# Seven head pairs' outputs turned by transposing DMAs instead of TensorE transposes, and rounding splits dealt to other engines

## The chip, the cores and the metric

One NeuronCore of one Trainium2 chip runs the kernel, with its five engines: TensorE (PE, with its weight loads as PEld), VectorE (DVE), ScalarE (ACT), GpSimd (POOL) and SyncE (SP). SP computes nothing here: it issues all of the kernel's DMAs, one after the other. The metric is the device time of one execution in microseconds. Lower is better.

## The reference

Three stages follow each other: attention whose mask lets a query see only the keys of its own cluster, a token and channel mixer, and a second mixer with cosine and sine. The inputs are in single precision.

```python
mask = q_assign[:, :, :, None] == k_assign[:, :, None, :]     # argmax over 16 centroids per head
scores = np.where(mask, scale * q @ k.T, -1e9)
attn = softmax(scores)                                        # B=2, H=8, S=768, D=64
x = (attn @ v).transpose(0, 2, 1, 3).reshape(B, S, H * D)     # B, 768, 512
# moe
h = np.maximum(x.transpose(0, 2, 1) @ w_tok1, 0.0) @ w_tok2   # 768 -> 256 -> 768, over the tokens
u = x + h.transpose(0, 2, 1)
x = u + np.maximum(u @ w_ch1, 0.0) @ w_ch2                    # 512 -> 1536 -> 512, over the channels
# moe2
theta = x @ w_theta
zr, zi = x * np.cos(theta), x * np.sin(theta)
y = einsum('ts,bsd->btd', w_tok_r, zr) + einsum('ts,bsd->btd', w_tok_i, zi)
u = x + y
out = u + np.maximum(u @ w_ch, 0.0)
```

## The kernel before

Products of single precision are made from three matmuls (`mm3`, L174): each operand is split into a high part, rounded to the format that TensorE multiplies fast, and a low part that holds the rest. The product is high by low, low by high and high by high, summed in PSUM. So every operand that a matmul reads has to be rounded (the "h" tile) and subtracted (the "l" tile) by some engine first. `split_sb` (L129) does this from SBUF: its fourth argument names the engine that rounds ("p" POOL at L132, "v" DVE, "a" ACT at L136) and its fifth the engine that subtracts ("p" POOL, otherwise DVE, at L138). A two-letter word such as "av" or "pp" in the code is such a choice. `load_w` (L152) loads a weight of 512 KB that comes as 64-bit numbers, rebuilds single precision from it on ACT (L161), DVE (L164, L165) and POOL (L168, `k_f<-k_f,k_raw` and the like), and splits it. Without a choice of its own a weight is rounded by POOL and ACT in turn and subtracted by POOL.

**Attention.** The 16 heads are taken in eight pairs. A head has three units of two query tiles of 128 rows, so there are 48 units, and the program's loop (L580) goes over them: the scores of unit n (`scores`, PE L491 and L492, then the maximum on DVE and the exponential on ACT), the transposes of unit n-1 (`turn`, L511) and the products with v of unit n-2 (`values`, L532). The outcome is written transposed, channels by tokens, into a tile `xt` (128 channels of a pair by 768 tokens). `natural` (L545) turns it into tokens by channels: six PE transposes (L555, tile `x`) of `xr`, a copy of `xt`, and six multiplications on DVE (L558) that read PSUM and divide by the softmax sums `ri`. `xr` is a copy made by a DMA (`exact`, L124, at L126), from SBUF to SBUF. `natural` runs three units after a pair's last values.

Meanwhile the operands of the heads ahead are made. For a pair, q and k are loaded (`load_pair`), POOL scales q (L438) and splits both (tag "hl", four buffers, so the next pair's split waits until the DMAs that read the last one are through). For each head SP then copies the parts into the shape that the scores need (`prep`, L465): `qh<-qh` twice, `q<-ql`, `k<-kh` twice, `k<-kl`. The cluster masks come as rows 64 to 79 of the second operands `q2` and `k2` (`place`, L450: `q<-m`, `k<-m`, four of 16 rows). In the trace and the lists below q_0, k_0 are those of even heads, q_1, k_1 of odd ones. `qh` and the masks have their buffers back only when the last scores of the head two before are through, so for an even head SP begins about 13.5 us ahead of the first score that needs all of it.

**Between attention and the mixers.** The token mixer needs `nat(b, s)`, the attention's output by tokens, split (`tok_x`, L184, tiles `xh`, `xl`), and the channel mixer needs it transposed. For this `spread` (L205) separates the 16-bit halves of each number (`halves`, L100, tile `xp`), stores them to DRAM (L116, `xtd<-xp`), and `gather` (L211, L214) reads them back with a transposing DMA (DMA_TRANSPOSE, `xc<-xtd`). `tok_up` (L191) makes g and its parts gh (ACT) and gl (DVE, L200), `tok_down` (L219) makes h and adds it to x. `u_split` (L693) splits the result for the channel mixer. The weights of the second mixer's token matmuls are loaded by `load_tok` (L816), 18 of them, named k; products with them are `y`.

**What sets the order.** The program says which tile is made from which. The order of the instructions on each engine, SP's queue included, comes out of a scheduler that simulates the time of every instruction and is fixed when the kernel is built. On the chip each engine works through its list in that order, and an instruction that has to wait holds back all that stand behind it on that engine.

Of the kernel before, what the change touches and what calls it, by code (L numbers as in the profile page):

```python
# [20 lines left out]
P = 128  # L21
# [14 lines left out]
X_AT = (29, 31, 33, 35, 37, 39)  # L36
# [23 lines left out]
def tile_model(ctx: ExitStack, tc: tile.TileContext, qT, kT, v, cent, w1, w2, wc1, wc2, wth, wri, wch, out):  # L60
# [20 lines left out]
    identr = const.tile([P, P], F32R, name="identr")  # L81
    nc.vector.tensor_copy(out=identr, in_=ident)
# [40 lines left out]

    def exact(t, x):  # L124

        nc.sync.dma_start(out=t.bitcast(F32), in_=x)  # L126
        return t
# [106 lines left out]
    with ExitStack() as actx:  # L234
# [235 lines left out]
        xts, xrs = {}, {}  # L470
# [74 lines left out]
        def natural(b, pr):  # L545

            last = (b, pr) == (B - 1, H // 2 - 1)
            sm, xt = sums[b, pr], (xts if last else xrs)[b, pr]
            ri = small.tile([P, NT, 2], F32, tag="ri", bufs=2, name=f"ri{b}{pr}")
            nc.vector.tensor_scalar(out=ri, in0=sm, scalar1=1e-9, scalar2=None, op0=ALU.add)  # L550
            nc.vector.reciprocal(out=ri, in_=ri)
            for q0, n in ((0, 4), (4, 2)):
                ps = ps_t.tile([P, 4, P], F32 if last else F32R, tag="t", name=f"x{b}{pr}{q0}")
                for i in range(n):
                    nc.tensor.transpose(ps[:, i, :], xt[:, (q0 + i) * P : (q0 + i + 1) * P], ident if last else identr)  # L555
                ps = ps.bitcast(F32)
                for i in range(n):
                    nc.vector.tensor_tensor(  # L558
                        out=nat(b, q0 + i)[:, pr * P : pr * P + P].rearrange("p (h d) -> p h d", h=2),
                        in0=ps[:, i, :].rearrange("p (h d) -> p h d", h=2),  # L560
                        in1=ri[:, q0 + i, :].unsqueeze(2).to_broadcast([P, 2, D]),
                        op=ALU.mult,
                    )
# [16 lines left out]
        for n in range(len(units) + SKEW):  # L580
# [42 lines left out]
            if 0 <= n - SKEW:  # L623
# [6 lines left out]
                if h % 2 == 1 and u == NT // 2 - 1:  # L630
                    late.append((n + 3, b, h // 2))
                    if n - SKEW < len(units) - 1:
                        xrs[b, h // 2] = exact(ap.tile([P, S], F32R, tag="xr", bufs=1, name=f"xr{b}{h}"), xts[b, h // 2])
# [27 lines left out]
        for s in range(NT):  # L661
            tok_x(1, s, part, ("av", "ap")[s % 2])
# [30 lines left out]
    def u_split(ch, c):  # L693

        us[ch, c] = h, l = block(f"uh{ch}{c}"), block(f"ul{ch}{c}")
        l = split_sb(h, l, xc[ch][:, c, :], "a", "v")
# [119 lines left out]
    def load_tok(t):  # L816
        wts[t] = [load_w(wri[t][:, j * 512 : j * 512 + 512], f"k{t}{j}") for j in range(2 * NT // 4)]
# [162 lines left out]
```

## Time and profile before

| what | value |
|---|---|
| median of 3 runs | 643.3 us (642.75 to 644.39) |
| the profiled execution | 642.99 us |
| its span | 641.3 us |
| PE busy | 629.2 us (98%) |
| DVE busy | 411.4 us (64%) |
| ACT busy | 356.1 us (56%) |
| POOL busy | 298.1 us (46%) |
| granted clock of TensorE | 9 tenths or more in all 40 slices of the span |
| chain of work that ended last | PE 85%; POOL 4%; DVE 4%; issue 3% |

The span is the stretch from the first to the last instruction that the profile holds; the execution's own time lies 1.7 us above it. Busy times are sums over the span, so an engine with a low share can still be the one that is late in one place. The chain is followed back from the last instruction through what released each step. In the timelines the number in brackets at the end of a row is the time for which the engine had stood idle before that row, and what ended this.

### The profile page before, as it was taken

What the parts mean: (1) busy time and instruction counts of PE and PEld (TensorE: products, weight loads), DVE (VectorE), ACT (ScalarE), POOL (GpSimd) and SP (SyncE); (2) the same over time, 40 slices, a digit from 0 to 9 for tenths busy, and PEclk for the clock granted to TensorE, in tenths of its full rate; (3) what the DMA queues carried; (4) which work ended last, traced back from release to release, by engine and by line L of the source; (5) the groups of instructions that cost most, each with busy time, mean ns of one, the idle gap of its engine ahead of it and who ended that gap; (6) DMA issues with size and microseconds to landing.
All of it is one profiled execution on the core that took longest, in us unless ns stands there. A gap on an engine that the chain in (4) does not pass through costs nothing.

```text
span 641.3 us, 9886 instructions
## 1 busy us (share of the span) xinstructions
PE 629.2 (98%) x3510; PEld 503.7 (79%) x3510; DVE 411.4 (64%) x653; ACT 356.1 (56%) x670; POOL 298.1 (46%) x261
## 2 busy tenths in 40 slices
PE   8999999999999999899999999999999999999997
PEld 6777787777777767788888888888888877888886
DVE  6877777778787758776565442464668977645222
ACT  6766777677778857456433510455767964422110
POOL 8330312309341115437776521492976998644000
PEclk9999999999999999999999999999999999999999
DMA  8655667454698315724433310636061236652331
GB/s 302 171 147 136 173 139 181 120 145 112 182 226 172 108 34 198 163 67 132 132 131 102 127 36 20 177 99 164 2 164 34 85 109 184 182 147 68 88 105 55
DMA packets 65762, 82.02 MB, mean 128 GB/s; under 512 B 40816, under 2 KB 44080, under 8 KB 65712
## 3 DMA queue, kind: packets, MB, share of 16 engines
q1 hardware_dynamic: 65712, 81.39, 46.6%
q8 instruction: 28, 0.46, 0.3%
q14 instruction: 22, 0.18, 0.1%
HBM read 39.65 MB, written 12.06 MB: 81 GB/s over the span
## 4 chain that ended last, share of the span: by engine, by line
PE 85%; POOL 4%; DVE 4%; issue 3%; ACT 2%; DMA 1%; ACTq 0%; POOLq 0%
PE o L532 10%; PE t L511 10%; PE s L491 5%; PE c L180 5%; PE c L178 5%; PE r L178 5%; PE s L492 5%; PE r L180 5%; PE r L179 5%; PE c L179 5%; PE y L178 4%; PE y L180 4%; PE y L179 4%; PE po L179 2%; PE po L180 2%
## 5 line engine op out<-in xcount | busy, mean ns | idle before, releaser
L494 DVE TENSOR_REDUCE nm<-s 128x1 f32<-128x768 f32 x96 | 90.4, 950 | 16.1 <-PE s L492 15.4
L496 ACT ACTIVATE e<-s,nm 128x768 f32<-128x768 f32 x96 | 86.6, 904 | 24.6 <-DVE nm L494 24.2
L511 PE MATMUL t<-ident,e 128*128 128x128 f32 x576 | 84.1, 276 | 0.7 <-ACT e L496 0.4
L511 PEld LDWEIGHTS t<-ident,e 128*128 128x128 f32 x576 | 66.9, 140 | 17.6 <-ACT e L496 6.1
L491 PE MATMUL s<-k,qh 128*128 128x384 f32 x188 | 71.7, 381 | 0.6 <-ACT e L496 0.5
L532 PE MATMUL o<-p,vs 128*64 128x256 f32 x564 | 71.2, 388 | 0.0
L514 ACT ACTIVATE p<-t 128x512 f32<-128x512 f32 x96 | 52.8, 595 | 27.7 <-PE t L511 27.6
L492 PE MATMUL s<-k,q 128*128 128x384 f32 x192 | 64.5, 338 | 0.2 <-ACT k L355 0.2
L178 PE MATMUL y<-zl,k_h 128*128 128x512 f32 x144 | 56.5, 392 | 1.4 <-POOL k_h L132 1.1
L180 PE MATMUL y<-zh,k_h 128*128 128x512 f32 x144 | 56.0, 389 | 0.0
L179 PE MATMUL y<-zh,k_l 128*128 128x512 f32 x144 | 56.0, 389 | 0.0
L179 PE MATMUL r<-uh,c_l 128*128 128x512 f32 x144 | 56.0, 389 | 0.0
L180 PE MATMUL r<-uh,c_h 128*128 128x512 f32 x144 | 55.9, 389 | 0.0
L178 PE MATMUL r<-ul,c_h 128*128 128x512 f32 x144 | 55.4, 389 | 0.0
L532 PEld LDWEIGHTS o<-p,vs 128*64 128x64 f32 x564 | 36.3, 136 | 22.8 <-issue 7.0
L168 POOL TENSOR_TENSOR c_f<-c_f,c_raw 128x512 uint32<-128x512 uint32 x24 | 32.5, 1354 | 40.8 <-issue 19.7
L179 PE MATMUL c<-rh,c_l 128*128 128x512 f32 x128 | 49.8, 389 | 0.0
L180 PE MATMUL c<-rh,c_h 128*128 128x512 f32 x128 | 49.6, 389 | 0.0
L178 PE MATMUL c<-rl,c_h 128*128 128x512 f32 x128 | 49.5, 389 | 0.0
L779 ACT ACTIVATE rh<-r 128x512 fp32r<-128x512 f32 x36 | 20.5, 592 | 49.1 <-PE r L180 49.0
L780 DVE SCALAR_TENSOR_TENSOR rl<-r,rh 128x512 fp32r<-128x512 f32 x36 | 24.4, 687 | 27.4 <-ACT rh L779 27.2
L132 POOL TENSOR_SCALAR qh<-ql 128x768 fp32r<-128x768 f32 x7 | 5.8, 835 | 74.4 <-DMA qh<-qh 70.9
(223 smaller groups left out, 1468.1 us busy)
## 6 DMA issues: line engine op xcount, KB each, us to landing
c_raw<-wc SPq DMA_DIRECT2D x24, 512.0 KB, 3.4
k_raw<-wri SPq DMA_DIRECT2D x18, 512.0 KB, 3.8
qh<-qh SPq DMA_DIRECT2D x28, 192.0 KB, 3.1
k<-kh SPq DMA_DIRECT2D x28, 192.0 KB, 4.1
ql<-qT SPq DMA_DIRECT2D x8, 384.0 KB, 3.2
kl<-kT SPq DMA_DIRECT2D x8, 384.0 KB, 3.7
vs<-v SPq DMA_DIRECT2D x16, 192.0 KB, 2.4
w_raw<-w SPq DMA_DIRECT2D x6, 512.0 KB, 4.1
```

The lines of the kernel that those rows point to most:

```text
L168: nc.gpsimd.tensor_tensor(out=wu, in0=wu, in1=lo, op=ALU.add)
L178: nc.tensor.matmul(ps, ah, bl, start=first and i == 0, stop=False)
L179: nc.tensor.matmul(ps, al, bh, start=False, stop=False)
L180: nc.tensor.matmul(ps, ah, bh, start=False, stop=last and i == n - 1)
L491: nc.tensor.matmul(ps[:, half, :NH], qh[:, c], k1[:, n], start=True, stop=False)
L492: marks["scores"] = nc.tensor.matmul(ps[:, half, :NH], ql[:, c], kk[:, n], start=False, stop=True)
L494: marks["max"] = nc.vector.tensor_reduce(out=nm, in_=ps[:, :, :NH], axis=AX.XY, op=ALU.max, negate=True)
L496: marks["exp"] = nc.scalar.activation(out=e.rearrange("p (a n) -> p a n", a=2), in_=ps[:, :, :NH], func=AF.Exp, bias=nm, accum_out=sums[b, ...
L511: marks["turn"] = nc.tensor.transpose(ps[:, a, i * P : i * P + P], es[i][:, kt * P : kt * P + P], ident)
L514: marks["pA"] = nc.scalar.activation(out=p, in_=ps, func=AF.Copy)
L532: nc.tensor.matmul(po[r : r + 64, :], vs[:, kt, :], pr[kt // 2][:, kt % 2, :], start=kt < 2, stop=kt >= NT - 2, tile_position=(0, r),)
L780: nc.vector.scalar_tensor_tensor(out=l, in0=ps, scalar=0.0, in1=h.bitcast(F32), op0=ALU.max, op1=ALU.subtract)
```

## The change

1. Seven of the eight pairs (all but the last) no longer use PE for `natural`. POOL separates the 16-bit halves of `xt` (`halves` with "p", tile `xh`, 128 x 1536 elements of 16 bits, after's L109), SP stores them to DRAM (`xd<-xh`, after's L114), and in the next turn of the loop at the earliest a transposing DMA reads them back as `xr`, now tokens by channels (`turned_back`, after's L118). The six multiplications by `ri` read `xr` from SBUF and are done by POOL (after's L553). `natural` runs six units after the pair's last values. `xr` has two buffers instead of one.
2. `tok_x` of batch 0 is called for the units 32, 33, 35, 37, 39, 41 (before: 29, 31, 33, 35, 37, 39).
3. In the second batch's `tok_x` DVE subtracts for all six tiles; before, POOL did it for three of them.
4. `u_split` of the first four column tiles (ch 0) subtracts on POOL instead of DVE.
5. The 18 weights of `load_tok` are rounded on ACT and subtracted on DVE; before, nine were rounded by POOL and nine by ACT, and POOL subtracted all 18.

```diff
--- before.py
+++ after.py
@@ -33,7 +33,7 @@
 RAW = 4
 HL = 4
 
-X_AT = (29, 31, 33, 35, 37, 39)
+X_AT = (32, 33, 35, 37, 39, 41)
 GATHERS = (4, 5, 0, 1, 2, 3)
 SPREAD_AT = (43, 44, 45, 46, 47, 48)
 W1_AT = {41: "pp", 43: "pp", 46: "av"}
@@ -78,8 +78,6 @@
     marks = {}
     ident = const.tile([P, P], F32, name="ident")
     make_identity(nc, ident)
-    identr = const.tile([P, P], F32R, name="identr")
-    nc.vector.tensor_copy(out=identr, in_=ident)
     NCH = B * NT // 4
     xc = [const.tile([P, 4, DM], F32, name=f"xc{i}") for i in range(NCH)]
 
@@ -120,11 +118,6 @@
         nc.sync.dma_start_transpose(
             out=t.bitcast(U16).rearrange("p (c q) -> p c q", c=n), in_=rows.rearrange("p t n -> (p t) n")
         )
-
-    def exact(t, x):
-
-        nc.sync.dma_start(out=t.bitcast(F32), in_=x)
-        return t
 
     def split_sb(h, l, x, rnd, sub):
 
@@ -467,7 +460,7 @@
             return qh, q2[i], k1, k2[i], load_v(b, h)
 
         sums = {}
-        xts, xrs = {}, {}
+        xts, xrs, stored = {}, {}, []
 
         def scores(b, h, u, ops):
 
@@ -550,12 +543,14 @@
             nc.vector.tensor_scalar(out=ri, in0=sm, scalar1=1e-9, scalar2=None, op0=ALU.add)
             nc.vector.reciprocal(out=ri, in_=ri)
             for q0, n in ((0, 4), (4, 2)):
-                ps = ps_t.tile([P, 4, P], F32 if last else F32R, tag="t", name=f"x{b}{pr}{q0}")
+                if last:
+                    ps = ps_t.tile([P, 4, P], F32, tag="t", name=f"x{b}{pr}{q0}")
+                    for i in range(n):
+                        nc.tensor.transpose(ps[:, i, :], xt[:, (q0 + i) * P : (q0 + i + 1) * P], ident)
+                else:
+                    ps = xt.rearrange("p (i n) -> p i n", n=P)[:, q0:, :]
                 for i in range(n):
-                    nc.tensor.transpose(ps[:, i, :], xt[:, (q0 + i) * P : (q0 + i + 1) * P], ident if last else identr)
-                ps = ps.bitcast(F32)
-                for i in range(n):
-                    nc.vector.tensor_tensor(
+                    (nc.vector if last else nc.gpsimd).tensor_tensor(
                         out=nat(b, q0 + i)[:, pr * P : pr * P + P].rearrange("p (h d) -> p h d", h=2),
                         in0=ps[:, i, :].rearrange("p (h d) -> p h d", h=2),
                         in1=ri[:, q0 + i, :].unsqueeze(2).to_broadcast([P, 2, D]),
@@ -628,9 +623,17 @@
                         values(group)
                     group = []
                 if h % 2 == 1 and u == NT // 2 - 1:
-                    late.append((n + 3, b, h // 2))
+                    late.append((n + 6, b, h // 2))
                     if n - SKEW < len(units) - 1:
-                        xrs[b, h // 2] = exact(ap.tile([P, S], F32R, tag="xr", bufs=1, name=f"xr{b}{h}"), xts[b, h // 2])
+                        k = f"{b}{h}"
+                        t = halves(ap.tile([P, S], F32, tag="xr", bufs=2, name=f"xh{k}"), xts[b, h // 2], "p")
+                        rows = dram.tile([P, 2, S], U16, tag="xd", bufs=2, name=f"xd{k}")
+                        store(rows, t, nc.sync)
+                        stored.append((n + 1, (b, h // 2), rows))
+            if stored and n >= stored[0][0]:
+                _, k, rows = stored.pop(0)
+                xrs[k] = ap.tile([P, S], F32, tag="xr", bufs=2, name=f"xr{k[0]}{k[1]}")
+                turned_back(xrs[k], rows, NT)
             while late and (n >= late[0][0] or n == len(units) + SKEW - 1):
                 _, b, pr = late.pop(0)
                 natural(b, pr)
@@ -659,7 +662,7 @@
                 ps = ps_o.tile([P, 512], F32, tag="o", name=f"g0{t}")
             tok_up(0, t, ps, lambda name: ap.tile([P, S], F32R, tag="raw", bufs=RAW, name=name)[:, :512])
         for s in range(NT):
-            tok_x(1, s, part, ("av", "ap")[s % 2])
+            tok_x(1, s, part, "av")
         split = marks["h"], marks["l"]
         for s in GATHERS:
             spread(1, s, ap.tile([P, S], F32, tag="hl", bufs=HL, name=f"xp1{s}")[:, :DM], "a")
@@ -693,7 +696,7 @@
     def u_split(ch, c):
 
         us[ch, c] = h, l = block(f"uh{ch}{c}"), block(f"ul{ch}{c}")
-        l = split_sb(h, l, xc[ch][:, c, :], "a", "v")
+        l = split_sb(h, l, xc[ch][:, c, :], "a", "p" if ch == 0 else "v")
         turned[ch] = marks["h"], l
 
     for c in range(NC):
@@ -814,7 +817,7 @@
     wts = {}
 
     def load_tok(t):
-        wts[t] = [load_w(wri[t][:, j * 512 : j * 512 + 512], f"k{t}{j}") for j in range(2 * NT // 4)]
+        wts[t] = [load_w(wri[t][:, j * 512 : j * 512 + 512], f"k{t}{j}", "av") for j in range(2 * NT // 4)]
 
     plan = []
     for t in range(B * NT):
```

Three places in the order of the instructions. A transposing DMA takes a place in SP's list where a plain copy stood. On SP, around the preparation of head 6, the first of the fourth pair (tiles qh, k: first operands; q_0, k_0: second ones; m: masks), the list before has:

```order
L465 DMA qh_1574<-qh_1348 64x768
L126 DMA xr_1446<-xt_936 128x768
L465 DMA qh_1574<-qh_1348 64x768
L465 DMA q_0_145<-ql_1349 64x768
L465 DMA k_1575<-kh_1353 64x768
L465 DMA k_0_147<-kh_1353 64x768
L465 DMA k_1575<-kl_1354 64x768
L450 DMA q_0_145<-m_1523 16x384 x2
L450 DMA k_0_147<-m_1523 16x384 x2
L450 DMA q_1_146<-m_1523 16x384
```

The same stretch of SP's list after the change:

```order
L458 DMA qh_1568<-qh_1329 64x768 x2
L458 DMA q_0_143<-ql_1330 64x768
L458 DMA k_1569<-kh_1334 64x768
L458 DMA k_0_145<-kh_1334 64x768
L458 DMA k_1569<-kl_1335 64x768
L114 DMA xd_1429<-xh_1427 128x1536
L443 DMA q_0_143<-m_1517 16x384 x2
L118 DMA_TRANSPOSE xr_1493<-xd_1429 128x6x256
L443 DMA k_0_145<-m_1517 16x384 x2
L443 DMA q_1_144<-m_1517 16x384
```

The copy to `xr` is gone from among the `qh`; the store `xd` stands behind `k<-kl`, and the DMA that turns it back stands between the two masks of the even head. It reads what the store wrote. Four even heads have this pattern.

The second place is SP's list for head 14, the first of the last pair. Before:

```order
L465 DMA qh_2723<-qh_2489 64x768
L126 DMA xr_2587<-xt_2065 128x768
L465 DMA qh_2723<-qh_2489 64x768
L465 DMA q_0_145<-ql_2490 64x768
L465 DMA k_2724<-kh_2494 64x768
L465 DMA k_0_147<-kh_2494 64x768
L465 DMA k_2724<-kl_2495 64x768
L450 DMA q_0_145<-m_2668 16x384 x2
L450 DMA k_0_147<-m_2668 16x384 x2
```

After, behind two `qh` and one `q_0<-ql`:

```order
L458 DMA k_2702<-kh_2459 64x768
L458 DMA k_0_145<-kh_2459 64x768
L114 DMA xtd_3114<-xp_3112 128x1024
L207 DMA_TRANSPOSE xc_66<-xtd_2941 128x4x256
L207 DMA_TRANSPOSE xc_66<-xtd_3008 128x4x256
L114 DMA xtd_3179<-xp_3177 128x1024
L443 DMA q_0_143<-m_2646 16x384 x2
L443 DMA k_0_145<-m_2646 16x384 x2
L443 DMA q_1_144<-m_2646 16x384
L114 DMA xtd_3214<-xp_3212 128x1024
L207 DMA_TRANSPOSE xc_66<-xtd_3061 128x4x256
L458 DMA k_2702<-kl_2460 64x768
```

`k<-kl`, the last of the six copies that the head's first score reads, has moved behind three stores, three transposing DMAs and five masks. Before, the gathers stood ahead of the head's copies or behind its masks.

The third place is DVE around the second batch's `gl` (L200). Before:

```order
L164 TENSOR_SCALAR c_0_raw<-c_0_f 128x512
L165 SCALAR_TENSOR_TENSOR c_0_f<-c_0_f,c_0_raw 128x512
L138 TENSOR_TENSOR ul_3499<-xc_68,uh_3498 128x512
L138 TENSOR_TENSOR ul_3503<-xc_68,uh_3502 128x512
L138 TENSOR_TENSOR ul_3507<-xc_68,uh_3506 128x512
L138 TENSOR_TENSOR ul_3511<-xc_68,uh_3510 128x512
L164 TENSOR_SCALAR c_1_raw<-c_1_f 128x512
L165 SCALAR_TENSOR_TENSOR c_1_f<-c_1_f,c_1_raw 128x512
L200 SCALAR_TENSOR_TENSOR gl_3534<-g_3514,gh_3533 128x512
```

After:

```order
L131 TENSOR_TENSOR xl_3357<-rest,xh_3356 128x512
L131 TENSOR_TENSOR xl_3361<-rest,xh_3360 128x512
L157 TENSOR_SCALAR c_0_raw<-c_0_f 128x512
L158 SCALAR_TENSOR_TENSOR c_0_f<-c_0_f,c_0_raw 128x512
L157 TENSOR_SCALAR c_1_raw<-c_1_f 128x512
L158 SCALAR_TENSOR_TENSOR c_1_f<-c_1_f,c_1_raw 128x512
L193 SCALAR_TENSOR_TENSOR gl_3504<-g_3484,gh_3503 128x512
```

The four `ul` have left DVE's list, and `gl` follows the weight's rebuilding at once. On POOL's list they stand around the same weight's addition (L168, after's L161).

## Rows read from the trace of the kernel before

**Rows 1.** The page's busy times: engine, busy us, share of the span, instructions.

```profile
PE 629.2 (98%) x3510; PEld 503.7 (79%) x3510; DVE 411.4 (64%) x653; ACT 356.1 (56%) x670; POOL 298.1 (46%) x261
```

**Rows 2.** Busy times by stretch, one pair of heads: stretch and its length, us (instructions), clock, DMA.

```profile
143.19:170.51 27.32, 27.32 (x209) 21.02 (x208) 21.92 (x38) 20.30 (x43) 18.64 (x18) 1.00 0.55 137
```

**Rows 3.** Waits of PE: us in total, times, longest.

```profile
PE h L179 <- DVE gl L200: 2.1, 1, 2.1
PE h L178 <- DVE w_l L138: 1.5, 2, 0.9
...
PE y L178 <- POOL k_h L132: 1.1, 1, 1.1
...
PE y L178 <- POOL zl L138: 0.3, 1, 0.3
```

**Rows 4.** Groups of instructions by line and form, L555: ns min/median/max, first and last start.

```profile
L555 PE MATMUL x<-identr,xr x42: 223/250/282, 60.5 to 223.3; 128*128 128x128 f32 x42
```

**Rows 5.** Timeline of PE: the sixth pair's output transposes, and head 14's first score.

```profile
197.76 0.71 PE L555 MATMUL x<-identr,xr 128*128 128x128 f32 x6
198.31 0.41 PE L511 MATMUL t<-ident,e 128*128 128x128 f32 x2
...
199.39 0.42 PE L491 MATMUL s<-k,qh 128*128 128x384 f32 x1
```

**Rows 6.** Groups by line and form, L138 and L111: subtractions and half copies.

```profile
L138 POOL TENSOR_TENSOR k_l<-k_f,k_h x18: 1285/1298/1789, 463.5 to 594.9; 128x512 fp32r<-128x512 f32 x18
L138 DVE TENSOR_TENSOR ul<-xc,uh x12: 681/686/1819, 258.4 to 278.0; 128x512 fp32r<-128x512 f32 x12
...
L138 POOL TENSOR_TENSOR kl<-kl,kh x7: 1829/1834/1842, 19.1 to 181.9; 128x768 fp32r<-128x768 f32 x7
...
L111 POOL COPY xp<-xc x6: 1027/1042/1366, 155.8 to 183.7; 128x1024 uint16<-128x1024 uint16 x6
```

**Rows 7.** Timeline of POOL: the first step of a pair's split.

```profile
121.86 0.84 POOL L132 TENSOR_SCALAR qh<-ql 128x768 fp32r<-128x768 f32 x1 [18.40 <-DMA qh<-qh]
```

**Rows 8.** Timeline of SP: preparation of head 6, first of the fourth pair.

```profile
103.92 0.50 SPq L465 DMA_DIRECT2D qh<-qh  x1
...
108.16 1.15 SPq L465 DMA_DIRECT2D k<-kl  x1
109.41 1.75 SPq L450 DMA_DIRECT2D q<-m  x2
111.20 1.22 SPq L450 DMA_DIRECT2D k<-m  x2
```

**Rows 9.** DMAs of L126 and of L465: us from issue to landing.

```profile
L126 SPq DMA_DIRECT2D xr<-xt x7: 516/548/588, 47.6 to 214.6; - x7
...
DMA to landing us min/median/max: 2.8/3.7/6.1
...
L465 SPq DMA_DIRECT2D k<-kl x14: 596/886/1150, 24.6 to 206.1; - x14
...
DMA to landing us min/median/max: 2.5/3.9/6.1
```

**Rows 10.** The page's DMA issues: KB each, median us to landing.

```profile
k<-m SPq DMA_DIRECT2D x30, 24.0 KB, 2.6
```

**Rows 11.** Timeline of SP: preparation of head 14.

```profile
192.03 0.89 SPq L465 DMA_DIRECT2D k<-kl  x1
...
196.81 0.53 SPq L116 DMA_DIRECT2D xtd<-xp  x1
197.39 3.10 SPq L214 DMA_TRANSPOSE xc<-xtd  x2
```

**Rows 12.** Timeline of DVE: the four ul ahead of gl.

```profile
258.35 5.14 DVE L138 TENSOR_TENSOR ul<-xc,uh 128x512 fp32r<-128x512 f32 x4
```

**Rows 13.** Busy times by stretch, columns as in rows 2, where the second mixer begins.

```profile
490.00:500.00 10.00, 10.00 (x50) 8.22 (x49) 9.55 (x16) 8.99 (x18) 10.00 (x8) 1.00 0.20 72
```

## The prediction

> **What bounds the kernel now.** I read the busy times first: TensorE is busy 98% of the span [rows 1], so only what shortens its work or its few gaps can gain, and every wait that comes new to it is paid in full. The stretches by time say where there is room: while a pair of heads goes through, PE is busy for all of 27.32 us and DVE for 21.92, even in the stretch where POOL works 18.64 us [rows 2]. So work put on POOL there is cheap as long as nothing waits for it. PE's waits come next: 2.1 us for `gl` and 1.5 for `w_l` between attention and the channel mixer, 1.1 for `k_h` and 0.3 for `zl` at the second mixer [rows 3], 5.0 together of what can be won back. Last I read SP's timeline, because the change puts waits into the one list that all DMAs share [rows 8, 11].
>
> **PE's transposes (part 1).** 42 transposes go [rows 4]. They are pipelined, so their busy time overcounts; six of them start at 197.76 and the next work starts at 198.31 [rows 5], 0.55 us. Seven groups: **-3.9 us**. The bounds are 0.55 and 0.71 a group (the busy time of the same row), 3.9 and 5.0. I take the lower, for it is the distance of two starts.
>
> **What POOL gets for it.** Per pair a half copy of 128x1536 and six multiplications of 128x128. The copy of 128x1024 takes 1.04 us [rows 6], so this one about 1.6. POOL's two-input operations take 1.83 us for 768 columns and 1.30 for 512 [rows 6], which falls by 0.27 for every 128 columns; for 128 that leaves 0.3 to 0.65 (the line drawn on, and half of 512), I take 0.46, 2.8 for six. In all 4.4 us a pair. It is hidden: POOL waits 18.40 us for its next pair's split, until the copies that read the last split are through [rows 7]. Gone, that cover would cost the later start of the split, up to 4.4 us a pair, but the split is done before SP can copy it. I cost POOL's work at nothing. That DVE is relieved of its 42 multiplications gives nothing either, since PE does not wait for DVE there [rows 3].
>
> **SP: masks of four even heads.** The copy to `xr` (0.55 us to issue, 0.6 with the gap [rows 9]) goes; a store and a DMA that turns it back come, and the second cannot start until the first has landed. Call t the moment at which SP may begin with an even head, 103.92 for head 6 [rows 8]. The `k<-kl` is out at 109.31, t+5.4, less 0.6 is t+4.8. The store starts there; from the nearest row of its size, `xr<-xt`, it lands 2.8, 3.7 or 6.1 us later [rows 9], by the median at t+8.5. The two `q<-m` (1.75) fit in between. The turning DMA's issue costs 1.55 for four blocks (3.10 for two such [rows 11]), so 2.3 for six: t+10.8. The first `k<-m` lands 2.6 us later [rows 10], t+13.4, the second, half of 1.22 on, at t+14.0. Head 14's first score starts at 199.39 [rows 5]; three periods of 27.32 before is 117.43, t+13.5, the masks' own matmuls some 0.3 and 0.6 later, and 0.55 comes off for the dropped transposes: t+13.2 and t+13.5. So PE waits some 0.5 us, four times: **+2.0**. Bounds: none with 2.8 and an issue of 1.55, 2.9 each with 6.1.
>
> **SP: head 14.** Its `k<-kl` now stands behind three stores, three gathers and five masks. From t, SP needs 3.65 us for what stood ahead before (108.16 less 103.92 less 0.6), 1.8 for three stores at 0.53 and gaps, 4.65 for three gathers, 3.7 for the masks (1.75, 1.22, half of 1.75 and gaps): it is issued at t+13.8. It lands 2.5, 3.9 or 6.1 us later [rows 9]; being behind small masks, with only 24 KB each [rows 10], I take 3.2, between 2.6 for these and the median. t+17.0 against a need at t+13.5 less 0.55: **+4.0**, bounds 3.3 and 6.9. In the kernel before it was issued at 192.03 [rows 11], 7.4 us ahead of the score.
>
> A rule stands against this price: the Trainium skill (Advanced Engine Details and Errata, section X-Bar Transpose (TRN2)) says that transposing DMAs are as fast as plain ones. The rows here differ, 1.55 us to issue against 0.53 for a plain store of the same 256 KB. By the rule head 14 would wait about 0.9 and the masks not at all, and the sum would be near 635.7.
>
> **Between attention and the channel mixer (parts 2 to 4).** `gl` stood behind four `ul` of 5.14 us on DVE [rows 12]; they go to POOL. Three more `xl` come to DVE ahead of it, 0.69 each like the median `ul` [rows 6] or 1.29 like these four (5.14/4), so `gl` comes 1.3 to 3.1 us earlier where 2.1 are wanted. The weights' rebuilding (`w_l`) starts earlier against PE in the new order, with the last values ahead of g's matmuls; of its two waits I leave the shorter, 0.6 (1.5 less 0.9), standing. Of 3.6 [rows 3] that is **-3.0**, bounds -1.0 (`gl` gains only 1.3 and a new wait of 0.3 comes) and -3.6. On POOL the first channel weights now stand among four `ul` at 1.30; PE has g's and h's matmuls ahead of their use, so I cost this at nothing, at most 3.9 (three `ul`), which the range holds.
>
> **The second mixer (part 5).** POOL loses 18 subtractions at 1.30 [rows 6] and nine roundings; DVE gets 18 at 0.69, 12 us in all, ACT nine roundings. POOL is busy all of 490 to 500, but DVE has 9.55 of 10 too [rows 13]: DVE is late next. PE's 1.4 us [rows 3] should nearly go: **-1.3**, bounds -1.4 and +3 (four subtractions of 0.69 that land ahead of PE's need).
>
> **The sum** on the profiled execution: 642.99 - 3.9 + 2.0 + 4.0 - 3.0 - 1.3 = 640.8. The median of the runs lies 0.3 above that execution, so **641.1**. A measurement of this kernel can tell 0.3% from no change, 1.9 us: faster means under 641.4.
>
> **Rivals.**
> - *Fast: SP issues the turning DMAs as quickly as stores.* With 0.53 us in place of 1.55 for each of the three gathers, head 14 waits 3.1 less, and with 0.8 in place of 2.3 (six blocks) no mask is late: 641.1 - 3.1 - 2.0 = 636.0, and with every wait of SP hidden 635.1. For it: the two gathers [rows 11] went out while the queue was full, so that their 3.10 may hold waiting. Against: the plain store just ahead of them took 0.53. It is what the rule named above says of this kernel. Partly true it gives up to 638.5.
> - *Slower: SP held by the store.* One mechanism: the turning DMA waits for its store's landing, with the masks and everything later behind it in SP's list. It decides from 1.0 us more at each of the four even heads on, a landing of 4.7 instead of 3.7: 641.1 + 4 x 1.0 = 645.1, where slower begins at 643.3 + 1.9 = 645.2. At 6.1 it is 641.1 + 4 x 2.4 = 650.7. For it: copies of this size did take 6.1 [rows 9], among the same loads. Against: the median.
> - *DVE late at the second mixer:* the +3 in place of -1.3, 645.4. For it: DVE's 9.55 of 10; against: the weights' splits need not go out in that stretch.
> - *The change does not do what it says:* no, the lists show all its parts moved.
>
> **How the numbers follow.** Forecast 0.40, its own range 638.6 to 643.6, of which 0.22 is faster and 0.18 within 0.3%. Fast rival 0.25, all faster. SP held 0.20, all slower. DVE late 0.15, 0.08 slower, 0.07 the same. Faster 0.47, same 0.25, slower 0.28. The range runs from the fast rival's 635.1 to 647.0, which leaves out the upper half of SP held and little else.
>
> **What would show it.** No PE transposes before the last pair, and a pair's period of 26.8 us. In PE's waits, `s` waiting for DMAs `k<-m` about 0.5 us each at heads 2, 4, 6 and 8, and for `k<-kl` 4 us at head 14. No wait for `gl`; DVE's share up, POOL's down in 490 to 560. The forecast is wrong if head 14 starts on time, if the masks' waits exceed 1.5, or if a new wait for `c_h`, `c_l` or `k_l` shows up.

## The result and the profile after

The change makes the kernel faster by about 0.9%: 637.6 us in the median of six runs (637.03 to 639.65) against 644.0 of the kernel before beside it (642.75 to 645.12), a ratio of 0.9909 with a 95% interval of 0.9888 to 0.993. The forecast was 641.1; the direction was right and the range held the time, but the gain is 6.4 us where 2.2 were forecast.

The profiled execution shown here took 639.65 us (span 637.9), the slowest of the six. A second profiled execution of the same kernel, in the run after_again below, took 638.16 (span 636.5); it gives the same picture, and both stand in the tables. The granted clock of TensorE is 1.00, its upper level of 2.4 GHz, in both. Part of the spread of the runs goes with this clock: executions of the kernel before at 0.996 or 0.997 took 644.2 to 645.8 us, those at 0.999 or 1.00 took 643.05 in the median.

The page's busy times, after; they answer to [rows 1]:

```profile
PE 628.5 (99%) x3468; PEld 502.4 (79%) x3468; DVE 405.4 (64%) x627; ACT 357.7 (56%) x679; POOL 292.3 (46%) x284
```

Forty-two PE instructions fewer and a span that is 3.4 us shorter, and yet PE's busy time falls by only 0.7 us: busy time is a poor gauge of where the time went. The starts on PE's timeline are the better one. Five marks divide the program: the first and the last score (`s<-k,qh` at L491, after's L484; the very first unit has lines of its own and is left out), the first and the last matmul of the channel mixer's `r` (`r<-ul,c_h`), and the last of the end (`po<-ch_l,u3h`).

| stretch, us | forecast change | before | after | after_again | change |
|---|---|---|---|---|---|
| start to first score | 0 | 14.73 | 15.50 | 14.76 | 0.0 to +0.8 |
| first to last score (attention) | +2.1 | 210.82 | 211.30 | 211.27 | +0.5 |
| last score to first r | -3.0 | 47.08 | 43.63 | 42.82 | -3.5 to -4.3 |
| first r to last r | 0 | 200.63 | 200.63 | 200.68 | 0 |
| last r to last po | -1.3 | 164.28 | 163.08 | 163.13 | -1.2 |

So the gain is made between attention and the channel mixer and at the second mixer, about where the forecast had it. What it missed is the attention, which was to lose 2.1 us and lost 0.5.

The waits of PE that last 0.2 us or more between the last score and the first r, after (engine, line, what it waits for: us in total, times, longest); [rows 3] has the largest of before:

```profile
PE g L171 <- DVE xl L131: 1.7, 1, 1.7
PE o L525 <- DVE xt L534: 0.3, 1, 0.3
```

`gl` and `w_l`, 3.6 us before, are gone. A wait for `xl`, which DVE now subtracts, has come; it is 0.9 in after_again. From the last r on, the waits of after are these:

```profile
PE po L172 <- DVE u3l L135: 0.6, 1, 0.6
PE x2t L738 <- DVE xc L797: 0.2, 1, 0.2
```

`k_h` and `zl` (1.4 in [rows 3]) are gone, and DVE is waited for in their place, 0.8 together. The stretch 490 to 560 (busy us of PE, PEld, DVE, ACT and POOL, then clock, DMA share and GB/s, as in [rows 2]), before and then after:

```profile
490.00:560.00 70.00, 68.34 (x304) 55.17 (x303) 53.65 (x71) 44.28 (x79) 62.77 (x49) 1.00 0.43 128
```

```profile
490.00:560.00 70.00, 69.33 (x308) 56.47 (x308) 53.10 (x80) 46.14 (x84) 43.81 (x32) 1.00 0.44 132
```

POOL falls from 62.77 to 43.81 us. DVE, feared to be late there, is no busier in this stretch: its 18 `k_l` are spread from 458.8 to 592.5.

**Attention.** A pair of heads can be timed from one `sim` group to the next, which PE runs once a pair (start us, duration, then engine, line, operation, tiles). Before, two pairs running, and after:

```profile
97.61 0.52 PE L325 MATMUL sim<-ql,cst 128*32 128x384 f32 x2
...
124.93 0.52 PE L325 MATMUL sim<-ql,cst 128*32 128x384 f32 x2
```

```profile
97.45 0.52 PE L318 MATMUL sim<-ql,cst 128*32 128x384 f32 x2
...
124.72 0.52 PE L318 MATMUL sim<-ql,cst 128*32 128x384 f32 x2
```

A pair took 27.32 us and takes 27.27. The transposes worth 0.55 a pair are no longer there, but hardly any time went with them. At the start of head 14 PE waits, as forecast, but for 1.2 us and not 4.0:

```profile
200.43 1.52 PE L525 MATMUL o<-p,vs 128*64 128x256 f32 x12
203.13 0.41 PE L484 MATMUL s<-k,qh 128*128 128x384 f32 x1 [1.19 <-ACT w_f L154]
```

The releaser named is ACT, but the wait is for several semaphores, and `k<-kl`, which the score reads, is the late one: it lands at 203.04, and where it is issued earlier (kl_ahead below) the wait is gone. SP's timeline for this head, after (it answers to [rows 11]):

```profile
185.99 1.15 SPq L458 DMA_DIRECT2D qh<-qh  x2
187.24 0.54 SPq L458 DMA_DIRECT2D q<-ql  x1
187.87 1.39 SPq L458 DMA_DIRECT2D k<-kh  x2
189.35 0.87 SPq L114 DMA_DIRECT2D xtd<-xp  x1
190.27 3.72 SPq L207 DMA_TRANSPOSE xc<-xtd  x2
...
199.92 0.54 SPq L458 DMA_DIRECT2D k<-kl  x1
```

With SP's start at t = 185.99 it is issued at t+13.9, where the forecast had t+13.8; it lands 3.1 us later, and the score follows. No score waits for a mask.

### The profile page after: what moved, and what is told of

It reads as the page before. It is cut to its first block, busy times and chain, and to the rows that moved or that the text cites. A ratio compares the mean times of both kernels' runs of the same rounds, so it can differ in the third digit from the quotient of the medians.

```text
span 637.9 us, 9757 instructions
## 1 busy us (share of the span) xinstructions
PE 628.5 (99%) x3468; PEld 502.4 (79%) x3468; DVE 405.4 (64%) x627; ACT 357.7 (56%) x679; POOL 292.3 (46%) x284
## 4 chain that ended last, share of the span: by engine, by line
PE 82%; DVE 6%; DMA 4%; POOL 3%; ACT 2%; issue 2%; SPq 0%; ACTq 0%; POOLq 0%; DVEq 0%
PE o L525 9%; PE t L504 8%; PE s L484 6%; PE r L171 5%; PE r L173 5%; PE r L172 5%; PE c L171 5%; PE c L173 5%; PE s L485 5%; PE c L172 5%; PE y L173 4%; PE y L171 4%; PE y L172 4%; PE po L172 2%; PE po L173 2%
## 5 line engine op out<-in xcount | busy, mean ns | idle before, releaser
L504 PE MATMUL t<-ident,e 128*128 128x128 f32 x576 | 78.8, 273 | 0.3 <-ACT p L507 0.3
L484 PE MATMUL s<-k,qh 128*128 128x384 f32 x188 | 72.5, 386 | 1.3 <-ACT w_f L154 1.2
L484 PEld LDWEIGHTS s<-k,qh 128*128 128x128 f32 x188 | 35.3, 188 | 19.4 <-ACT p L507 10.8
L161 POOL TENSOR_TENSOR c_f<-c_f,c_raw 128x512 uint32<-128x512 uint32 x24 | 32.0, 1336 | 34.5 <-issue 16.0
L161 POOL TENSOR_TENSOR k_f<-k_f,k_raw 128x512 uint32<-128x512 uint32 x18 | 25.6, 1424 | 43.1 <-DVE k_f L158 26.6
```

Of the source, the lines that this page charges most:

```text
L161: nc.gpsimd.tensor_tensor(out=wu, in0=wu, in1=lo, op=ALU.add)
L484: nc.tensor.matmul(ps[:, half, :NH], qh[:, c], k1[:, n], start=True, stop=False)
L504: marks["turn"] = nc.tensor.transpose(ps[:, a, i * P : i * P + P], es[i][:, kt * P : kt * P + P], ident)
```

## The experiments

Each kernel was timed beside the kernel before. "Pair" is the distance of two `sim` groups in the middle of the attention (in no_turn_on_pe, of the two between which PE waits for nothing). The stretches are those of the table above, from one profiled execution each; before has 210.8, 47.1, 200.6 and 164.3.

| run | median us | ratio to before (95%) | pair | attention | last score to first r | first r to last r | last r to last po |
|---|---|---|---|---|---|---|---|
| after_again | 638.1 | 0.9903 (0.9885 to 0.9921) | 27.28 | 211.3 | 42.8 | 200.7 | 163.1 |
| part1_alone | 643.6 | 1.0004 (0.9985 to 1.0023) | 27.28 | 211.0 | 46.1 | 200.6 | 165.0 |
| splits_alone | 641.5 | 0.9961 (0.9946 to 0.9976) | 27.32 | 210.8 | 44.9 | 202.2 | 163.5 |
| no_turn_on_pe | 651.1 | 1.0110 (1.0081 to 1.0138) | 27.37 | 223.1 | 44.8 | 200.6 | 164.9 |
| two_of_six | 643.2 | 0.9987 (0.9974 to 1.0) | 26.96 | 209.5 | 47.2 | 200.6 | 164.3 |
| kl_ahead | 641.4 | 0.9962 (0.9947 to 0.9976) | 27.28 | 213.2 | 44.5 | 200.6 | 163.1 |
| old_order | 647.4 | 1.0048 (1.003 to 1.0066) | 26.95 | 217.5 | 43.7 | 201.1 | 163.0 |
| old_order_kl_ahead | 641.4 | 0.9963 (0.9951 to 0.9976) | 26.95 | 211.1 | 45.0 | 203.8 | 163.1 |
| without_part5 | 640.8 | 0.9958 (0.9944 to 0.9972) | 27.28 | 211.4 | 42.3 | 200.7 | 166.1 |
| without_parts3_4 | 641.9 | 0.9970 (0.9958 to 0.9981) | 27.28 | 211.5 | 46.5 | 200.6 | 163.1 |
| old_order_kl_dve | 642.2 | 0.9977 (0.9964 to 0.9991) | 26.95 | 211.4 | 45.1 | 202.5 | 163.1 |
| old_order_halves | 643.1 | 0.9995 (0.998 to 1.001) | 26.95 | 215.3 | 43.7 | 202.0 | 163.1 |

### The same kernel again

No edit.

> The changed kernel once more, unaltered, for a second profile. Its runs fell at 637.0 to 637.7 and at 639.5 to 639.7 us, and the profile was of one at 639.65, in which the first full score began at 15.5 us against 14.7 before. Theory 'first loads': the 2 us between the two groups come from before 25 us and from the one wait at head 14; a profile at 637 shows the first score near 14.7 and less wait there. Rival: the two groups differ somewhere after attention; then the marks up to 180 us stand as in the first profile. Ratio 0.988 to 0.993 in both.

It took 638.1 us, as the result had it. The first score comes at 14.8 instead of 15.5, so half of the difference between the two profiled executions (1.5 us) lies ahead of it; head 14 waits 1.22 again, against the expectation of less, and the wait for `xl` is 0.8 shorter. Before's first score was early too (14.7), while splits_alone and two_of_six, whose programs begin like it, had 15.53 and 15.45: this is a scatter that no part of the change makes.

### Part 1 by itself, and the splits by themselves

part1_alone takes parts 3 to 5 back out of the changed kernel, so that parts 1 and 2 are left (part 2 was not tried apart from part 1):

```diff
-            tok_x(1, s, part, "av")
+            tok_x(1, s, part, ("av", "ap")[s % 2])
...
-        l = split_sb(h, l, xc[ch][:, c, :], "a", "p" if ch == 0 else "v")
+        l = split_sb(h, l, xc[ch][:, c, :], "a", "v")
...
-        wts[t] = [load_w(wri[t][:, j * 512 : j * 512 + 512], f"k{t}{j}", "av") for j in range(2 * NT // 4)]
+        wts[t] = [load_w(wri[t][:, j * 512 : j * 512 + 512], f"k{t}{j}") for j in range(2 * NT // 4)]
```

splits_alone makes the same three lines' change, the other way round, in the kernel before.

> Only the outputs' way through DRAM and the later token splits of batch 0; the three dealings of splits are undone. Its list on TensorE is that of the changed kernel. Theory 'order': the seven pairs gain next to nothing, because the list in which TensorE now takes the same work needs 4.36 us a unit instead of 4.31, so the pair's period stays near 27.28 (27.32 before); with 1.2 us of wait at head 14 the attention part ends later by 0.3 (0.9 less 1.2), and what remains of gain lies between attention and the channel mixer: 0 to -2 us in all. Rival 'price': a pair gains 0.55 us, and the dealt-out splits hid it: -3 us or more here.

> Only the three dealings of splits; outputs are turned on TensorE as before, and TensorE's list is that of the kernel before. If the gain between attention and channel mixer (3.4 us in the profile) and at the second mixer (1.2 us) comes from the dealings: -3.5 to -4.6 us, no wait for gl and none for k_h. Rival: the 3.4 us come from POOL's and DVE's lists being freed by the pairs' new way: only -1 to -2 us, with the waits for w_l still there.

Turning the outputs by DMA, with the later token splits of part 2, is worth nothing alone (1.0004, within 0.2% either way). The splits alone give 0.4%, and both together 0.97%, more than the sum. PE's waits behind attention say why. part1_alone:

```profile
PE g L171 <- POOL xl L131: 1.9, 1, 1.9
PE h L172 <- DVE gl L193: 0.4, 1, 0.4
```

splits_alone:

```profile
PE h L178 <- DVE w_l L138: 1.5, 2, 0.9
PE r L178 <- DVE ul L138: 1.2, 1, 1.2
```

With part 1 alone `gl` is nearly in time already, but PE waits for POOL's `xl`. With the splits alone `gl` is in time, but `w_l` stays and `ul`, now late, comes new, 4 us after the first r. Each half takes away waits that the other would leave.

### The transposes left out

no_turn_on_pe leaves the transposes of seven pairs out of the kernel before (the outputs are not turned); DVE multiplies `xr` straight from SBUF:

```diff
-                for i in range(n):
-                    nc.tensor.transpose(ps[:, i, :], ...)
-                ps = ps.bitcast(F32)
...
+                    ps = xt.bitcast(F32).rearrange("p (i n) -> p i n", n=P)[:, q0:, :]
```

> The kernel before with the seven pairs' transposes left out on TensorE and nothing in their place: VectorE multiplies the copied tile as it lies, so the attention's output of seven pairs enters the mixers unturned. No store, no turning DMA, no work for POOL. TensorE's list in attention is then that of the changed kernel. Theory 'order': a pair still takes 27.28 us, the whole -0.3 to -1 us. Rival 'price': a pair takes 26.77 us, -3.9 us; then in the changed kernel the stores, DMAs or POOL slow TensorE.

It is 1.1% slower and no measure of the transposes: DVE's multiplications now wait for the DMA into `xr` and hold all that stands behind them on DVE, and PE waits for that:

```profile
197.91 0.90 DVE L560 TENSOR_TENSOR xc<-xr,ri 128x128 f32<-128x128 f32 x4 [5.15 <-DMA xr<-xt]
```

```profile
PE t L511 <- DVE oh L350: 8.1, 5, 4.5
```

It did show something else. In the attention PE's list came out in the order that it has after the change, and the one pair that no such wait touches takes 27.37 us, near the changed kernel's 27.27 and far from the 26.8 that the forecast wanted, without any turning DMA. That points to the order. So two_of_six keeps one transpose in each of the two groups (the other outputs are not turned), and PE's list keeps the order of before:

```diff
-                for i in range(n):
+                few = n if last else 1
+                for i in range(few):
...
-                        in0=ps[:, i, :].rearrange("p (h d) -> p h d", h=2),
+                        in0=ps[:, i % few, :].rearrange("p (h d) -> p h d", h=2),
```

> The kernel before with only two of each pair's six transposes on TensorE (seven pairs; VectorE multiplies the first of each group for all its columns, so attention's output is not the reference's). Its list on TensorE is otherwise that of the kernel before, in the same order: 28 transposes less and nothing else. Theory 'order' (a transpose costs TensorE its 0.092 us as long as the order stays; the change lost this by the new order): a pair takes 26.95 us instead of 27.32, the whole -2.6 us. Rival 'free': the transposes fill gaps that stay anyway; a pair stays at 27.3 us, the whole within 0.5 us of before.

A pair takes 26.96 us, 0.36 less for four transposes fewer: 0.09 each, and 0.55 for six, the forecast's price. The time falls by 0.13% only (the interval ends at no change), where 0.09 x 4 x 7 = 2.5 us would be 0.4%: PE gains a wait of 0.6 for DVE's multiplications, the stretch from the last `sim` group to the last score, without a wait in either, takes 46.3 us where it took 46.0 (why is open), so that the attention ends up 1.3 us shorter (209.5 against 210.8), and the first score came 0.7 later in this execution.

### The old order with part 1

old_order is the changed kernel with one PE transpose for each of seven pairs that nothing reads, and three copies on DVE, where `natural` stood before:

```diff
+                    gaps.append((n + 3, b, h // 2))
...
+            if gaps and n >= gaps[0][0]:
+                _, gb, gp = gaps.pop(0)
+                if (gb, gp) != (B - 1, H // 2 - 1):
...
+                            nc.tensor.transpose(gap[:, i, :], xts[gb, gp][:, q0 * P : q0 * P + P], ident)
+                        for i in range(3):
+                            nc.vector.tensor_copy(out=gap[:, 3, :], in_=gap[:, 0, :])
```

> The changed kernel plus, three units after each of seven pairs' last values, one transpose on TensorE and three copies on VectorE whose result nobody reads. With them TensorE's list in attention takes the kernel before's order (one transpose where six stood). Its SP list puts head 14's kl even later, behind the next head's first copies and a turning DMA. Theory 'order': a pair takes 26.86 us instead of 27.28, -2.5 us over the pairs; at head 14 TensorE waits 6 to 10 us, so the whole is 4 to 7 us over the changed kernel. Rival 'free': pairs at 27.3 us. Rival on SP's list: the wait there stays at 1 to 2 us.

Over the middle pairs PE's list is that of before again, but for the scores of two query tiles a pair that stand later, and a pair takes 26.95 us, 0.33 less than the changed kernel, with one transpose more. The turning DMAs are all there: it is the order, not they, that ate the saving. But the kernel is slower than before by 0.5%, for head 14:

```profile
209.45 0.66 PE L484 MATMUL s<-k,qh 128*128 128x384 f32 x1 [6.01 <-DMA k<-kl]
```

The wait costs more than its 6.01 us. The granted clock is 0.50 from 210 to 212 us, and a score that takes 0.34 us elsewhere takes 0.52 there; in after, where PE waits 1.19 at this place, it stays at 1.00. In no_turn_on_pe it is 0.50 from 200 to 205, behind the wait of 4.5.

Where the two orders differ can be seen on PE's timeline. A pair has six groups of products (`o`), and from one to the next a unit goes by. The six units of the pair around 100 us (start to start):

| unit | before | after | old_order |
|---|---|---|---|
| with the `sim` group | 5.09 | 5.29 | 5.10 |
| second | 4.33 | 4.37 | 4.32 |
| third, with a mask matmul (`pp`) | 4.44 | 4.55 | 4.44 |
| fourth | 4.33 | 4.35 | 4.33 |
| fifth; before with the six transposes, old_order with one | 4.82 | 4.35 | 4.43 |
| sixth | 4.31 | 4.36 | 4.32 |
| sum | 27.32 | 27.27 | 26.94 |

The fifth unit gains 0.47 by the change, and the other five lose 0.42. One unit of the changed kernel, from products to products:

```profile
118.01 1.52 PE L525 MATMUL o<-p,vs 128*64 128x256 f32 x12
119.45 0.44 PE L484 MATMUL s<-k,qh 128*128 128x384 f32 x1
...
120.27 0.82 PE L504 MATMUL t<-ident,e 128*128 128x128 f32 x6
120.84 0.42 PE L484 MATMUL s<-k,qh 128*128 128x384 f32 x1
...
121.62 0.82 PE L504 MATMUL t<-ident,e 128*128 128x128 f32 x6
122.37 1.52 PE L525 MATMUL o<-p,vs 128*64 128x256 f32 x12
```

It takes 4.36 us. Part of two units of old_order (the kernel before has the same groups from 107.21 on):

```profile
106.44 0.60 PE L504 MATMUL t<-ident,e 128*128 128x128 f32 x4
106.79 0.42 PE L484 MATMUL s<-k,qh 128*128 128x384 f32 x1
...
107.59 0.60 PE L504 MATMUL t<-ident,e 128*128 128x128 f32 x4
107.94 0.42 PE L484 MATMUL s<-k,qh 128*128 128x384 f32 x1
...
108.73 0.60 PE L504 MATMUL t<-ident,e 128*128 128x128 f32 x4
109.25 1.52 PE L525 MATMUL o<-p,vs 128*64 128x256 f32 x12
...
113.58 1.52 PE L525 MATMUL o<-p,vs 128*64 128x256 f32 x12
```

With 1.45 from the products to the next work the first is 4.26 us without its `pp`; the second, with groups of four and eight, is 4.33. The same twelve transposes hold up the next work for 0.35, 0.35 and 0.52 us in groups of four, 1.22 in all, and for 0.57 and 0.75 in groups of six, 1.32. That is the 0.1 between these two units; the others differ by 0.02 to 0.05, and the one with the `sim` group by 0.2. Why PE takes the new order longer is open.

### Head 14 in time

kl_ahead moves the half copies of the last three tiles from POOL to ACT, so that `k<-kl` comes earlier in SP's list; old_order_kl_ahead does the same in old_order:

```diff
-                spread(0, i, ap.tile([P, S], F32, tag="raw", bufs=RAW, name=f"xp0{i}")[:, :DM], "p")
+                spread(0, i, ap.tile([P, S], F32, tag="raw", bufs=RAW, name=f"xp0{i}")[:, :DM], "p" if i < 3 else "a")
```

> The changed kernel with the last three half copies of batch 0 on ScalarE instead of POOL, so that head 14's copy of kl stands ahead of the gathers in SP's list. TensorE's list in attention is unchanged. If the 1.2 us of wait at head 14 come from kl's place in SP's list, they go: -1.2 us against the changed kernel, ratio to the kernel before about 0.988, and the first score of head 14 follows without a wait. Rival: the wait moves on to another late transfer, 0 us.

> Both: the kernel before's order on TensorE kept by one unread transpose a pair, and the last three half copies of batch 0 on ScalarE, so that head 14's kl is issued ahead of its masks. Theory 'order' with the wait at head 14 gone: -2.5 and -1.2 us against the changed kernel, about 634 us, ratio to the kernel before 0.983 to 0.986. With SP's waits back as the prediction had them in this order (masks behind the turning DMA): 0.5 us at each even head. Rival 'free': no more than -1.2 us, ratio 0.988 or above.

In both head 14 starts on time, and both are slower than the change. kl_ahead: ACT's copy waits for a buffer that a store still reads, the exponentials stand behind it on ACT, and PE waits for them; behind attention it waits for ACT's `gh` too.

```profile
183.81 1.06 ACT L107 ACTIVATE xp<-xc 128x1024 uint16<-128x1024 uint16 x1 [1.33 <-DMA xtd<-xp]
```

```profile
PE s L484 <- ACT e L489: 2.2, 3, 1.2
PE h L171 <- ACT gh L192: 1.8, 2, 1.1
```

In old_order_kl_ahead the pairs keep 26.95, but waits of 2.0 for `w_l` between attention and the channel mixer and of 2.9 for `ul`, 6 us after the first r, take the gain. The copies on DVE in place of ACT ("v", old_order_kl_dve), or each copy's halves on POOL and DVE ("pv", old_order_halves), did no better:

> As old_order_kl_ahead, with the three half copies on VectorE in place of ScalarE. Pairs at 26.95 us, so 1.5 us earlier by the last sim than the changed kernel; no wait at head 14. What went wrong with ScalarE (2.9 us for ul and 2.0 for w_l behind attention) should not come from the half copies: if the order in attention is all that matters, those waits stay and the ratio is 0.995; if ScalarE's late list caused them, they go and the ratio is 0.985 to 0.988.

> As old_order_kl_dve, but each of batch 0's six half copies is shared, one half on POOL and one on VectorE. Pairs at 26.95 us. Head 14's copies stand behind four gathers in SP's list, so a wait of up to 2 us there if the prediction's price of a gather holds (1.33 us each measured), none if they are issued while SP is idle. Ratio 0.985 to 0.990, or 0.995 if ul and w_l are late again.

The first leaves `w_l` 2.0, `ul` 1.6 and a `p` of 1.4. In the second DVE's copy waits 2.26 us for a store's buffer, the maxima come late, PE waits 2.55 for an exponential, the granted clock is 0.50 from 178 to 180 us, and one pair takes 33.23; `ul` is 1.1 late as well. No kernel tried beat the changed one.

### The splits one by one

without_part5 takes the last line of part1_alone's edit out of the changed kernel, without_parts3_4 the first two.

> The changed kernel with the second mixer's weights split as before (nine rounded on POOL, all subtracted on POOL). If part 5 gained what its place showed, TensorE waits again 1.1 us for k_h and 0.3 for zl, and the stretch from the last r to the last po is 1.0 to 2.0 us longer than in the changed kernel (163.2; 165.0 with the pairs' new way alone): +1 to +2 us, ratio to the kernel before 0.992 to 0.994. The gap between the last score and the first r stays at 42.8 to 43.6. Rival: part 5 gains nothing by itself, 0 us.

> The changed kernel with the second batch's token splits and the first u_split dealt as before. If these dealings end the waits for g and h, the gap between the last score and the first r is 46.1 us again, as with the pairs' new way alone (42.8 in the changed kernel): +3 us, ratio to the kernel before 0.994 to 0.996, and TensorE waits some 1.9 us for POOL's xl and 0.4 for gl. Rival: the gap shortens with part 5 or by chance of the run: within 1 us of the changed kernel.

Part 5 is worth 3.0 us from last r to last po (166.1 against 163.1). Parts 3 and 4 are worth 2.9 to 3.7 between last score and first r (46.5 against 43.6 and 42.8): without them PE waits 2.2 for `xl` on POOL and 0.5 for `gl`. The longer waits are 1.1 to 1.9 of this; the rest was not traced.

## Why the prediction was right and wrong

On like executions the step is from 642.99 to 638.16, -4.8, where the sum had -2.2. The other 1.6 us of the measured -6.4 lie in the executions: before's profiled one was among its fastest, 1.0 under the median of 644.0 that its six runs had (the forecast knew three, and added 0.3), and 638.16 is 0.6 above the median of after. Of the 2.6 that the sum itself missed, the attention has 1.65 and the gap behind it 1.25; the end and the small stretches give 0.3 back. In the attention the sum was -3.9 + 2.0 + 4.0 = +2.1; measured are -1.1 up to the seventh `sim` group (151 us) and +1.6 from there on, 1.2 of it the wait at head 14. Without that wait the attention gained 0.8, so the transposes gave 0.8 and not 3.9, the masks cost nothing and not 2.0, and head 14 cost 1.2 and not 4.0. These errors of +3.1, -2.0 and -2.8 partly cancel, and that the time fell inside the range is in part luck.

- **PE's transposes, -3.9: right price, wrong saving.** The price of 0.55 us a group holds (two_of_six, 0.09 each). The step that failed is the one behind it, that the rest of PE's list stays as it is. It comes out of a scheduler, and without the transposes it came out in another order, in which the unit that had them gains 0.47 us and the other five of a pair lose 0.42. A pair gained 0.05 instead of 0.55, and its period is 27.27 where 26.8 was to show the forecast right; one early pair gained 1.0 (28.27 before, 27.27 after), half of it a wait of 0.5 for an exponential that is gone.
- **POOL's work, nothing: right.** The copy takes 1.46 us (forecast 1.6), six multiplications 2.19 (forecast 2.8; the line through 768 and 512 columns gives 0.49 for 128, not the 0.3 set beside it), and POOL then still stands idle 3.47 us ahead of its next split, in place of the 18.40 of [rows 7]:

```profile
116.80 2.19 POOL L553 TENSOR_TENSOR xc<-xr,ri 128x128 f32<-128x128 f32 x6 [12.24 <-DMA xr<-xd]
122.45 0.83 POOL L125 TENSOR_SCALAR qh<-ql 128x768 fp32r<-128x768 f32 x1 [3.47 <-DMA qh<-qh]
```

- **Masks of four even heads, +2.0: none.** SP's timeline after, beside [rows 8]. The head that begins here is head 8, the first of the fifth pair, by the count of PE's scores, and not head 6; the score at 117.43, three periods before head 14, is its own, so the times worked out stand. The four heads are 4, 6, 8 and 10, not 2 to 8.

```profile
103.81 1.15 SPq L458 DMA_DIRECT2D qh<-qh  x2
...
108.15 0.86 SPq L114 DMA_DIRECT2D xd<-xh  x1
110.25 1.18 SPq L443 DMA_DIRECT2D q<-m  x2
112.78 1.43 SPq L118 DMA_TRANSPOSE xr<-xd  x1
114.26 1.21 SPq L443 DMA_DIRECT2D k<-m  x2
```

  The store begins at t+4.3 (forecast 4.8), the turning DMA 4.6 behind it (3.7), and its issue takes 1.43 (2.3): the first `k<-m` is issued at t+10.5 where the sum gave t+10.8. The two land 2.7 and 2.2 us after their issues, at t+13.1 and t+13.3, ahead even of the forecast's needs at t+13.2 and t+13.5. The size that failed first is the issue, 2.3 against 1.43; the need moved too, as the next point shows.
- **Head 14, +4.0: 1.2.** Issue (t+13.9) and landing (3.1) came as worked out, though the terms for the masks add up to 3.85 and not 3.7. What failed is the need, t+12.95, which was read from the order of before. Before, three groups of products `o` lie between SP's start and head 8's first score (105.59, 110.03, 114.36, then the score at 117.43); after, a fourth stands ahead of the score (118.01, the score at 119.45), so that the score is wanted at t+15.6, and head 14's at 201.94, t+15.95. Against the old need `k<-kl` would have been 4.1 us late. So one error, the order, ate the saving of the first step and paid for most of this one.
- **The gap, -3.0: -3.5 to -4.3.** `gl` and `w_l` both went, where 0.6 of `w_l` was left standing; `xl` came for 0.9 to 1.7. Of the -4.3 in after_again the waits account for 3.0; the rest was not traced.
- **The second mixer, -1.3: -1.2.** Right. DVE was late by the 0.8 of `u3l` and `xc` and not by the 3 of the rival. But part 5 carries more than that: without it the changed kernel loses 1.8 us against before in this stretch (166.1 against 164.3), for `k_h` and `zl` keep PE waiting 1.4 as before and `u3l` 1.1 and `u3h` 0.3 come new.
- **The rivals.** The fast one named nearly the right time (636.0) for a wrong reason: the turning DMAs do not go out as stores do. The issues' rows, after (ns: min/median/max, first and last start):

```profile
L118 SPq DMA_TRANSPOSE xr<-xd x7: 1288/1441/1918, 58.3 to 222.6; - x7
...
L114 SPq DMA_DIRECT2D xd<-xh x7: 343/805/857, 54.9 to 219.7; - x7
```

  The Trainium skill (Advanced Engine Details and Errata, section X-Bar Transpose (TRN2)) calls the two equally fast. From issue to landing the trace agrees, 4.1 us for the turning DMA and 4.6 for the store in the median. But a turning DMA holds SP for 1.44 us in the median, against 0.81 for the store of the same 384 KB and 0.34 for the quickest one, and here the masks and copies stand behind it in the one list that SP issues. SP did stand behind the store (4.6 us from its start to the turning DMA, 6.1 at head 10), where the slower rival was to bite from 4.7 on, and no score waited: it is needed some 2 us later than the forecast had it.

## What to carry to other kernels

Where a scheduler makes the order, an operation that is taken away has no price of its own: read from the new list both when an operand is released and when it is wanted, and price the new order of the bound engine too. Two changes that each remove one of several waits close together have to be tried together, for alone either leaves or creates the wait that the other takes away. A copy whose buffer a DMA has to give back delays all that stands behind it on its engine: in the changed kernel it stands on POOL, for which PE waits nowhere in the attention, and PE did wait where it stood on ACT (kl_ahead) or DVE (old_order_halves).

## What the runs showed of the hardware that was not expected

- The same matmuls and transposes take PE 4.26, 4.33 or 4.36 us a unit by their order alone, at a granted clock of 1.00.
- Behind long waits of PE the granted clock is at the lower level, 1.2 GHz, for some us: 0.50 from 210 to 212 us in old_order (wait 6.0), from 200 to 205 in no_turn_on_pe (4.5), from 178 to 180 in old_order_halves (2.6). Such a wait costs more than its length.
- POOL's small multiplications of 128x128 take 0.40 us (median 399 ns), and six in a row 2.19, 0.37 each, below the 0.46 estimated from its larger operations; DVE takes 0.28 for the four of the last pair, out of PSUM:

```profile
L553 POOL TENSOR_TENSOR xc<-xr,ri x36: 394/399/910, 62.2 to 230.0; 128x128 f32<-128x128 f32 x36
...
L553 DVE TENSOR_TENSOR xc<-x,ri x4: 280/281/292, 238.3 to 238.9; 128x128 f32<-128x128 f32 x4
```

- A turning DMA of six blocks takes SP little longer to issue (1.44 us in the median) than one of four (1.30, `xc<-xtd`), where the forecast went by the number of blocks, 2.3 against 1.55. The 3.10 of the two in a row in [rows 11] are 1.34 and 1.23 with a pause between them.
